# Attention probabilities and values as fp16 parts in every tile, fewer turns by TensorE, and the second expert layer on four column groups

## Chip, cores and metric

The kernel runs on one core of a Trainium2 chip. The metric is the device time of one execution in microseconds (us); the time before is the median of three runs. One core has TensorE (PE; PEld is its load of weights), VectorE (DVE), ScalarE (ACT), GpSimd (POOL), and SyncE (SP), whose queue issues nearly all DMAs, in order. ACT's queue issues some.

## What is computed

Four batches of 576 tokens (2304 in all, 18 tiles of 128) pass through attention with a threshold, a dense layer pair, and a soft mixture of eight experts.

```python
scores = scale * np.matmul(q, k.transpose(0, 1, 3, 2))          # 4 batches, 8 heads, 576 x 576, depth 64
thresh = np.max(scores, axis=-1, keepdims=True) - tau
scores = np.where(scores >= thresh, scores, -1000000000.0)
attn = np.exp(scores - max); attn = attn / (sum + 1e-09)
x = attn @ v                                                    # 2304 x 512
h = x @ w_in; g = np.maximum(0.01 * h, h); x = g @ w_out        # 512 -> 2048 -> 512
logits = x @ phi                                                # 32 slots
slot_input = softmax(logits, 0).T @ x
for e in range(8): slot_out[e] = np.maximum(slot_input[e] @ w1[e], 0) @ w2[e]   # 512 -> 1024 -> 512
out = softmax(logits, 1) @ slot_out
```

## The kernel before

**How the program is ordered.** The code does not issue instructions directly. Each step is added to a plan with its engine or engines, an estimated duration, a priority (about the number of its tile), the buffers it reads and those it writes. A planner then places all steps in one order per engine, by its own estimate of when each can start; buffers are rings of fixed size (the table `O`: `AE`, `AH`, `AT`, `VX`, `VR` and so on are ring sizes, `DP`, `PO`, `PI`, `LH` shift priorities). On the chip each engine runs its list strictly in order. So a changed number in `O` or a changed estimate can move any step.

**Attention of a tile.** `attention(t)` handles 8 heads as 4 pairs. For a pair, `heads` multiplies q by k on PE in fp32 (L1100, two heads side by side on the two halves of the rows), DVE finds the row maxima (L1109) and the threshold (L1115), ACT applies a steep Prelu that drives all below the threshold far down (L1125, L1143). `ends` does the last 64 keys of all heads (L1071). Then there are two ways to get probabilities times values:

- `by_pe`: PE turns the pair's 9 blocks of 128x128 in fp32 (L1159), ACT takes the exponential out of PSUM (L1164), and PE multiplies by the fp32 values (L1176): 10 matmuls for a pair, each of which is two instructions in the trace.
- `by_dma`: ACT takes the exponential in place (L1192), DVE or ACT casts to fp16 (L1202, L1203), POOL writes the rest as a second fp16 part (L1213, three instructions), SP issues two transposing DMAs (L1226), and PE multiplies the fp16 parts by two fp16 parts of the values, `vx` (L1250): 28 matmuls for a pair.

`own` says which pairs go by PE: all four in tiles 0 to 3 (`P0`, `TP=4`), pair 3 in tiles 4 to 17 (`P1`). Tiles 4 and 13 straddle two batches, so their multiplications by values are issued twice. That makes 30 pairs by PE and 42 by DMA.

**The rest of a tile.** The result is scaled, turned (L1295) and split in two fp16 parts; `feed` multiplies by `w_in`, 48 matmuls a tile (L1331), ACT applies the leaky ReLU (L1343), DVE and POOL split the result (L1350, L1357), and four transposing DMAs a tile turn it (L1366) for the logits (L1376, L1380). `w_out` is not applied there: `w_out` times `phi` is made once, at the start (L846, L862), and the first transposing DMAs of `feed` wait for it. Every two tiles `block` adds to the sum over tokens (L1525). The weights arrive as 64-bit numbers and are converted by ACT, DVE and POOL in the first part of the program; values of each batch are scaled and split by `split_v`.

**The experts at the end.** The gather of the slots (L1641) reads `w_out` back from DRAM (16 loads in small buffers, the list `SM`). Then `w1` (32 chunks of 512 KB, L1685) and `w2` (32 chunks, L1753) stream in through the rings that attention no longer needs (`BIG`, 25 buffers here); a chunk's load waits until the matmuls that read the buffer before are done. In the first layer PE goes round the four column groups of 32 (`for j` inside), in the second it does one column group's four matmuls after the other. Then the output is multiplied out (L1785) and stored.

Of the kernel before, what the change touches and what calls it, by code (L numbers as in the profile page):

```python
# [359 lines left out]
def emit(tc, a, out, dbg=None, opt=None):  # L360
# [5 lines left out]
        LH=1.67, LB=3.5, HG=3, NR=6, NT=4, NW=3, XH=1, XT=2, VX=6, AE=2, AH=2, AT=3, QK=8, VS=5,  # L366
        VD=0.3, P0=(0, 1, 2, 3), P1=(3,), TP=4, TX=('eT', 'h'), VR=5, RAW=1, G=2, PO=-4.88,
        PI=-2.55, PV=-9, PK=-8.96, DA=-100, TJ=('rT', 'xT'), PS=0.0, NM=6, E=1, LA=2, MG=800,
        AL=0.44, MH=0, RES=0, MI=(1, 1, 1, 1), MO=(1, 1, 0, 0), WT=('w',), PST=0, BH=1, DP={'vr':
        1.76, 'xT': 0.1, 'xh': 0.34, 'X': 0.29, 'x32': 0.28, 'g': 0.0, 'E': -0.71, 'S0': -0.55,  # L370
        'S1': -1.0, 'h': 1.0, 'r': 1.06, 'rT': 0.34, 'ah': 0.5, 'vx': 0.32, 'misc': -0.82, 'dh':
        -0.87, 'z': -0.89, 'th': 0.68, 'aT': -1.0}, TU=('U', 'rT'), TO=('raw', 'rT'), TG=('g',),
        BI={'spa': 300}, LG=0.06, TE=0.16, NTS=1, WI=('w',), CAP=(), NA=23, QU=(), CX=('aT',),
        TW=('aT', 'g', 'xT'), E2=1, DT=200, TI=('r',), PJ=0.03, NU=2, SM=('vr', 'vx', 'rT', 'w',
        'w2', 'raw', 'x32', 'U'),
# [58 lines left out]
    for n, p_, k in (  # L434
# [4 lines left out]
        ("qk", "main", O["QK"]), ("vr", "main", O["VR"]), ("vx", "main", O["VX"]), ("vs", "main", O["VS"]),  # L439
# [36 lines left out]
    def dump(name, b, sel, prio=1e9):  # L476
        if dbg and name in dbg:
# [36 lines left out]
    gate8, rt = const([P, 1]), const([P, 1])  # L514
    dve_op(
        P0, 80,
        lambda: dve.tensor_scalar(
            out=gate8.ap, in0=gate.ap, scalar1=0.125, scalar2=None, op0=ALU.mult
        ),
        r=[gate], w=[gate8],  # L520
    )
    dve_op(
        P0, 80,
        lambda: dve.tensor_scalar(
            out=rt.ap, in0=taup.ap, scalar1=8.0, scalar2=None, op0=ALU.mult
        ),
        r=[taup], w=[rt],
    )
# [6 lines left out]
    )  # L535

# [289 lines left out]
    for c in range(FF // P):  # L826
# [21 lines left out]
        pe_op(PQ, 440, f, r=[w, ident], w=[tp])  # L848
# [15 lines left out]
        pe_op(PQ, 850, f, r=[wt, phi], w=[wpp])  # L864
# [102 lines left out]
    qk = {}  # L967

    def load_qk(b, prio, step):
        for pr in range(4):  # L970
            raw = qk[b, pr] = pl.buf("qk", [P, 2, KX])
            dma(
                prio + pr * step, t_dma(P * 2 * KX * 4),
                (lambda pr, raw: lambda dq: dq.dma_start(out=raw.ap, in_=a["qk"][b, pr]))(pr, raw), w=[raw],
            )

    vtiles, vfs, vrs_of = {}, {}, {}

    own = lambda t: O["P0"] if t < O["TP"] else O["P1"]
# [25 lines left out]
    def split_v(b, pr, prio, vr):  # L1005
        sv = svs[b]
        vf = lambda: vr.ap[:, :, 0:D]
# [10 lines left out]
        if any(pr not in own(t) for t in tiles_of(b)):  # L1018
            vx = vtiles[b, pr] = pl.buf("vx", [P, 2, 10, D + 2], F16)
            va = lambda w: vx.ap[:, w, :, 0:D]  # L1020
            q = prio + (O["VD"] if any(pr in own(t) for t in tiles_of(b)) else 0.0)
# [13 lines left out]
            fm = lambda eng: lambda: eng.memset(vx.ap[64:, 1, 8:, 0:D], 0.0)  # L1035
            add_alt(q, [("pool", 180, fm(pool)), ("dve", 110, fm(dve))], w=[(vx, 1)])
            for w in range(2):
                pool_op(
                    q, 100, (lambda w: lambda: pool.memset(vx.ap[:, w, :, D : D + 1], 1.0 - w))(w),
                    w=[(vx, 2 + w)],  # L1040
                )
        if any(pr in own(t) for t in tiles_of(b)):
            vs = vfs[b, pr] = pl.buf("vs", [P, 2, D + 2])
            fc = lambda eng: lambda: eng.tensor_copy(out=vs.ap, in_=vr.ap[:, 8:])
            add_alt(prio, [("pool", 300, fc(pool)), ("dve", 150, fc(dve))], r=[vr], w=[vs])
            fm = lambda eng: lambda: eng.memset(vr.ap[:, 0:8, D : D + 1], 1.0)
            add_alt(prio, [("pool", 100, fm(pool)), ("dve", 110, fm(dve))], w=[(vr, 1)])
            fm = lambda eng: lambda: eng.memset(vs.ap[:, :, D : D + 1], 1.0)
            add_alt(prio, [("pool", 100, fm(pool)), ("dve", 110, fm(dve))], w=[vs])
            for i in range(2):  # L1050
                fm = lambda eng, i=i: lambda: eng.memset(
                    vs.ap[64 - 64 * i : 128 - 64 * i, i, 0 : D + 1], 0.0)
                add_alt(prio, [("pool", 100, fm(pool)), ("dve", 110, fm(dve))], w=[vs])
            vrs_of[b, pr] = vr
# [8 lines left out]

    def ends(t, prio):
        Tp = pl.buf(("misc",), [P, H, KT], F32, "Tp")
        Ts, tn = pl.buf("T", [P, H, KT]), pl.buf("tn", [P, H])

        def f():
            for r0, r1, b, o in regs_of(t):
                for pr in range(4):  # L1070
                    pe.matmul(  # L1071
                        out=Tp.ap[r0:r1, 2 * pr : 2 * pr + 2], lhsT=qk[b, pr].ap[:, 0, o : o + r1 - r0],
                        rhs=qk[b, pr].ap[:, 1, KW:KX], start=(pr == 0), stop=True, skip_group_check=True,
                    )

        pe_op(prio, 900 * len(tile_parts(t)), f, r=[qk[b, pr] for b in tile_parts(t) for pr in range(4)], w=[Tp, Ts, tn])
        act_op(prio, t_act(512), lambda: act.activation(out=Ts.ap, in_=Tp.ap, func=AF.Copy), r=[Tp], w=[Ts])
# [5 lines left out]
        dve_op(  # L1083
            prio, 75,
            lambda: dve.tensor_scalar(
                out=tn.ap, in0=tn.ap, scalar1=rt.ap[:, 0:1], scalar2=None, op0=ALU.add
            ),
            r=[rt], w=[tn],
        )
        return Ts, tn  # L1090

    def heads(t, pr, prio, ae, flat, Ts, tn):
# [19 lines left out]
        for i in range(2):  # L1112
# [3 lines left out]
                    out=th.ap[:, i : i + 1], in0=nm.ap[:, i : i + 1], scalar1=rt.ap[:, 0:1],  # L1116
# [13 lines left out]
        tail = lambda: two(ae.ap[:, 2 * KW :]) if flat else ae.ap[:, :, KW:S]  # L1130
        pl.add(
# [15 lines left out]
    def by_pe(t, pr, p, parts, regs, Ts, tn, xa, xbuf):  # L1147
# [5 lines left out]
        def turn(c0, c1, key):  # L1153
# [3 lines left out]
            def f():  # L1157
# [11 lines left out]
        for i, (c0, c1) in enumerate(((0, 4), (4, 8), (8, 9))):  # L1169
            turn(c0, c1, i)  # L1170
# [698 lines left out]
```

## Time and profile before

| | us |
|---|---|
| median of three runs (lowest, highest) | 681.06 (677.28, 685.23) |
| the profiled execution: its time | 686.13 |
| its span, first to last instruction | 684.3 |
| PE, DVE, ACT, POOL busy in the span | 612.7, 406.3, 399.6, 172.8 |
| granted TensorE clock, mean of the span | 0.939 |

The span is read in five stages: up to 60 us loads and the first conversions; from 60 to about 205 us conversions beside the first four tiles; from there to 582 us the steady run of tiles; to 611 us the logits and gather of the last tiles; then the experts. A busy PE is not a PE at its peak, because matmuls overlap: what PE really needs is read from the distance between the starts of matmuls that follow each other at once.

### The profile page before, as it was taken

The page shows a single profiled execution, that of the slowest core. Times are in us where ns is not written, and L with a number is a line of the kernel's source. Part 1 is how long each engine was busy: PE and PEld are TensorE (multiplying, and loading weights), DVE is VectorE, ACT ScalarE, POOL GpSimd, SP SyncE. Part 2 cuts the span into 40 slices and gives each one's busy share as a digit, 9 for nine tenths or more (in the row PEclk, how much of TensorE's full clock was granted, in tenths as well). Part 3 has the DMA queues.
Part 4 walks back from the last instruction along what each step waited for, and adds up shares of the span by engine and source line. Part 5 has one row for each costly group of instructions (what it writes and reads, how often), then busy time and mean ns, then how long its engine had stood idle before and what let it go on. Part 6 is the DMA issues. An engine that isn't in the chain of part 4 may idle for free.

```text
span 684.3 us, 13565 instructions
## 1 busy us (share of the span) xinstructions
PE 612.7 (90%) x5212; PEld 369.2 (54%) x5212; DVE 406.3 (59%) x992; ACT 399.6 (58%) x745; POOL 172.8 (25%) x253
## 2 busy tenths in 40 slices
PE   4898887999879999999999898999999988489995
PEld 1666555776445656565555554655556643224552
DVE  3978869656757586599886555565767343310011
ACT  4887667776747677688786637576666522211022
POOL 0200100200323256245355323263363200200000
PEclk8798988999989999999999889999999999689997
DMA  8965410455998687899697659677669966839995
GB/s 321 375 221 181 129 61 17 139 159 164 163 214 152 115 143 127 186 190 200 121 177 119 114 89 201 132 133 131 105 123 213 203 131 177 267 109 413 409 408 215
DMA packets 203297, 123.94 MB, mean 181 GB/s; under 512 B 179168, under 2 KB 179680, under 8 KB 203232
## 3 DMA queue, kind: packets, MB, share of 16 engines
q1 hardware_dynamic: 199488, 114.02, 69.1%
q10 hardware_dynamic: 3744, 9.05, 5.5%
q8 instruction: 41, 0.67, 0.4%
q14 instruction: 24, 0.20, 0.1%
HBM read 70.48 MB, written 8.91 MB: 116 GB/s over the span
## 4 chain that ended last, share of the span: by engine, by line
PE 69%; ACT 11%; DVE 7%; DMA 6%; issue 3%; SPq 1%; POOL 1%; ACTq 0%; POOLq 0%; DVEq 0%
PE h L1331 23%; PE S L1100 9%; PE X L1176 6%; PE X L1753 6%; PE X L1250 5%; PE eT L1159 3%; PE misc L1176 3%; DMA aT<-ah 2%; ACT e L1164 2%; PE S L1685 2%; DMA rT<-r 2%; PE misc L1071 2%; PE misc L1525 2%; PE misc L862 2%; ACT g L1343 2%
## 5 line engine op out<-in xcount | busy, mean ns | idle before, releaser
L1331 PE MATMUL h<-wh,xT 128*128 128x512 f16 x864 | 215.0, 385 | 7.5 <-ACT g L1343 6.6
L1213 POOL TENSOR_TENSOR ah<-ae,ah 128x512 f16<-128x512 f32 (+1 forms) x126 | 120.6, 984 | 162.3 <-DVE ah L1202 130.7
L1331 PEld LDWEIGHTS <-xT 128*128 128x128 f16 x864 | 80.4, 100 | 101.7 <-issue 35.2
L1125 ACT ACTIVATE ae<-S,th 128x512 f32<-128x512 f32 x144 | 94.3, 686 | 17.5 <-POOL ah L1213 7.0
L1109 DVE TENSOR_REDUCE nm<-S 128x2 f32<-128x1024 f32 x72 | 87.7, 1219 | 28.2 <-PE S L1100 28.1
L1100 PE MATMUL S<-qk 64*128 64x512 f32 (+1 forms) x320 | 89.1, 690 | 9.6 <-DMA qk<-in_qk 5.9
L1343 ACT ACTIVATE g<-h,c 128x512 f32<-128x512 f32 x72 | 49.5, 687 | 70.0 <-PE h L1331 65.0
L1164 ACT ACTIVATE e<-eT,c,c 128x512 f32<-128x512 f32 (+1 forms) x90 | 60.1, 668 | 27.9 <-PE eT L1159 27.8
L1350 DVE CAST r<-g 128x512 f16<-128x512 f32 x57 | 27.8, 487 | 67.4 <-ACT g L1343 62.8
L1250 PEld LDWEIGHTS <-aT 128*128 128x128 f16 (+1 forms) x1344 | 49.7, 103 | 25.0 <-issue 14.6
L1250 PE MATMUL X<-vx,aT 128*128 128x65 f16 (+1 forms) x1344 | 54.4, 196 | 4.5 <-DMA aT<-ah 4.5
L1159 PE MATMUL eT<-c,ae 128*128 128x128 f32 x270 | 49.7, 296 | 8.7 <-ACT e L1164 8.1
L1192 ACT ACTIVATE ae<-ae,c,c 128x1152 f32<-128x1152 f32 x42 | 56.6, 1348 | 0.8
L1159 PEld LDWEIGHTS eT<-c,ae 128*128 128x128 f32 x270 | 34.1, 151 | 28.8 <-ACT e L1164 18.0
L1176 PE MATMUL X<-vr,e 128*128 128x65 f32 (+1 forms) x352 | 47.1, 281 | 0.0
L1357 DVE TENSOR_TENSOR r<-g,r 128x512 f16<-128x512 f32 x56 | 44.3, 791 | 3.9 <-ACT r L1352 3.0
L1134 POOL TENSOR_TENSOR ae<-T,th 128x128 f32<-128x128 f32 x33 | 15.4, 468 | 122.6 <-DVE th L1115 61.4
L1176 PEld LDWEIGHTS X<-vr,e 128*128 128x128 f32 (+1 forms) x352 | 45.0, 200 | 2.3 <-issue 1.2
L1202 DVE CAST ah<-ae 128x1152 f16<-128x1152 f32 x33 | 25.7, 779 | 20.2 <-ACT ae L1192 14.3
L1100 PEld LDWEIGHTS S<-qk 64*128 64x128 f32 (+1 forms) x320 | 23.2, 190 | 26.7 <-ACT ae L1125 7.8
L1115 DVE TENSOR_SCALAR th<-nm,c,tn 128x1 f32<-128x1 f32 x144 | 31.8, 264 | 0.8
L1376 PE MATMUL misc<-c,rT 128*128 128x64 f16 x288 | 19.1, 191 | 9.6 <-DMA rT<-r 9.2
(288 smaller groups left out, 911.0 us busy)
## 6 DMA issues: line engine op xcount, KB each, us to landing
wh<-in_w SPq DMA_DIRECT2D x21, 512.0 KB, 10.1
qk<-in_qk SPq DMA_DIRECT2D x15, 640.0 KB, 5.5
qk<-in_w SPq DMA_DIRECT2D x18, 512.0 KB, 8.0
r<-in_w_in SPq DMA_DIRECT2D x16, 512.0 KB, 4.1
r<-in_w SPq DMA_DIRECT2D x13, 512.0 KB, 10.2
rT<-in_w_out SPq DMA_DIRECT2D x25, 256.0 KB, 3.4
scr<-w SPq DMA_DIRECT2D x16, 256.0 KB, 3.3
vr<-in_v SPq DMA_DIRECT2D x9, 330.0 KB, 4.4
```

What stands on the lines that cost most here:

```text
L1100: pe.matmul(out=ps.ap[r0:r1, i], lhsT=qk[b, pr].ap[h, 0, o : o + r1 - r0], rhs=qk[b, pr].ap[h, 1, 0:KW], start=True, stop=True, skip_group ...
L1109: lambda: dve.tensor_reduce(out=nm.ap, in_=ps.ap, axis=AX.X, op=ALU.max, negate=True),
L1125: (lambda i: lambda: act.activation(out=main()[:, i], in_=ps.ap[:, i], func=AF.Prelu, bias=th.ap[:, i : i + 1], scale=1.0, alpha=2.0**90))(i),
L1159: pe.transpose(tp.ap[:, c - c0], ae.ap[:, c * P : (c + 1) * P], ident.ap)
L1164: lambda: act.activation(out=eT.ap[:, c0:c1], in_=tp.ap, func=AF.Exp, bias=nt.ap[:, 0:1], scale=gate8.ap[:, 0:1]),
L1176: pe.matmul(out=xa(2 * pr + i)[r0:r1], lhsT=eT.ap[:, c, r0:r1], rhs=(vfs[b, pr].ap[:, i] if c == 8 else vrs_of[b, pr].ap[:, c])[:, 0 : D + 1],
L1192: lambda: act.activation(out=ae.ap, in_=ae.ap, func=AF.Exp, bias=nt.ap[:, 0:1], scale=gate8.ap[:, 0:1]),
L1213: lambda: pool.tensor_tensor(out=ah.ap[:, h, w0 : w0 + c1 - c0], in0=ae.ap[:, h, c0:c1], in1=ah.ap[:, h, c0:c1], op=ALU.subtract),
L1250: pe.matmul(out=xa(2 * pr + i)[r0:r1], lhsT=w()[:, r0:r1], rhs=vtiles[b, pr].ap[:, wv, cv, 0 : D + 1], start=(n == 0 and 2 * pr + i in (0, ...
L1331: pe.matmul(out=hp.ap, lhsT=xT.ap[:, wx * 4 + k], rhs=wh(k, j, ww), start=(n == 0), stop=(n == 11),)
L1343: (lambda g, hp, j: lambda: act.activation(out=g.ap, in_=hp.ap, func=AF.Prelu, alpha=0.01, scale=hsc.ap[:, j : j + 1]))(g, hp, j),
L1357: fg = lambda eng, j, g: lambda: eng.tensor_tensor(out=r[j](1), in0=g.ap, in1=r[j](0), op=ALU.subtract)
```

## The change

1. Probabilities and values are now multiplied as fp16 parts in all pairs. `by_pe` has a new kind, "h": after the turn and the exponential, the result is cast to fp16 (DVE or ACT) and its rest is written as a second part (POOL or DVE), in three pieces; then 30 fp16 matmuls a pair (L1335 of the new file) replace the 10 in fp32.
2. Which pair goes which way: `K0='dhdh'` in tiles 0 to 3 (pairs 0 and 2 by DMA, 1 and 3 turned by PE), `K1=('dddd',)` in tiles 4 to 17 (all by DMA). So 8 pairs are turned by PE and 64 by DMA.
3. `split_v` makes `vx` for all pairs of all batches, the small tile `vh` for the "h" pairs, and no fp32 `vs` any more.
4. The second expert layer takes four chunks at a time and goes round the column groups in its inner loop.
5. Nine of the last sixteen chunks of `w1` are loaded as 18 halves into the small buffers (`SM`).
6. Ring sizes, priorities and some estimates changed. Code for splitting q and k in fp16 parts was added, but `QB=9` is above the highest batch, so it never runs (the options `QB`, `QR`, `HT` have no effect on what is computed).

```diff
-        LH=1.67, LB=3.5, HG=3, NR=6, NT=4, NW=3, XH=1, XT=2, VX=6, AE=2, AH=2, AT=3, QK=8, VS=5,
-        VD=0.3, P0=(0, 1, 2, 3), P1=(3,), TP=4, TX=('eT', 'h'), VR=5, RAW=1, G=2, PO=-4.88,
+        HT=0, HF=9, LH=1.9, LB=3.5, HG=3, NR=6, NT=4, NW=3, XT=2, VX=5, AE=2, AH=2, AT=3, QK=8,
+        VS=1, VD=0.52, TP=4, TX=('eT', 'h'), VR=4, RAW=1, G=3, PO=-6.45, PI=-0.91, PV=-8.22, PK=-9,
...
-    own = lambda t: O["P0"] if t < O["TP"] else O["P1"]
+    kind = lambda t, pr: (O["K0"] if t < O["TP"] else O["K1"][t % len(O["K1"])])[pr]
...
+        eh = pl.buf("ah", [P, 2, 9, P], F16)
+        for c0, c1, key in ((0, 4, 0), (4, 8, 1), (8, 9, 2)):
+            n = (c1 - c0) * P
+            pl.add(
+                p2,
+                [
+                    ("dve", P2(t_dve2(n)), lambda c0=c0, c1=c1: dve.tensor_copy(
+                        out=eh.ap[:, 0, c0:c1], in_=eT.ap[:, c0:c1])),
+                    ("act", t_act(n), lambda c0=c0, c1=c1: act.activation(
+                        out=eh.ap[:, 0, c0:c1], in_=eT.ap[:, c0:c1], func=AF.Copy)),
+                ],
...
+            fl = lambda eng, c0=c0, c1=c1: lambda: eng.tensor_tensor(
+                out=eh.ap[:, 1, c0:c1], in0=eT.ap[:, c0:c1], in1=eh.ap[:, 0, c0:c1], op=ALU.subtract)
...
+                todo = [(we, wv, c) for we, wv in ((0, 0), (0, 1), (1, 0)) for c in (*range(4 * i, 4 * i + 4), 8)]
...
+    def w1_of(e, k, late):
+        if not late:
+            w = load(a["w1"][e, k], T0 - 7, [P, 2, 512])
+            return [w, w], lambda n: w.ap[:, n]
+        w = [load(a["w1"][e, k][:, n], T0 - 7.5, [P, 512], "c2", SM, 512) for n in range(2)]
+        return w, lambda n: w[n].ap
...
-                for j in range(4):
-                    q = hts[G]
-
-                    def f(j=j, n=n, G=G, q=q, w=ws[j], hf=hf):
-                        for c in range(4):
+
+                def f(n=n, G=G, ws=ws, hf=hf):
+                    for c in range(4):
+                        for j in range(4):
                             pe.matmul(
```

**Where instructions stand, first place: PE in the first tile.** Before, these are a part of PE's list early in tile 0; `eT` is the turned pair, `S_77` the next pair's scores, `misc<-c_132,w` belongs to `w_out` times `phi`.

```order
L1159 MATMUL eT<-c_83,ae 128x128 x4
L1100 MATMUL S_77<-qk 128x512 x2
L1159 MATMUL eT<-c_83,ae 128x128
L1176 MATMUL X<-vr,e_183 128x65 x4
L1176 MATMUL X<-vs,e_183 128x65
L1176 MATMUL X<-vr,e_183 128x65 x4
L1176 MATMUL X<-vs,e_183 128x65
```

Now the same stretch of PE's list reads as follows (`aT` comes from a transposing DMA).

```order
L1206 MATMUL S_76<-qk 128x512 x2
L891 MATMUL misc<-c_136,w 128x32 x4
L1172 MATMUL misc<-qk 128x128 x4
L1278 MATMUL eT<-c_83,ae 128x128 x4
L1206 MATMUL S_77<-qk 128x512 x2
L875 MATMUL h<-c_83,w 128x128 x4
L1278 MATMUL eT<-c_83,ae 128x128 x4
L1411 LDWEIGHTS aT
L1411 MATMUL X<-vx,aT 128x65
```

The fp32 products are gone; the first product of tile 0 now waits in PE's list for a transposing DMA, behind the scores of three later pairs and beside `w_out` times `phi`.

**Second place: SP's list during the conversions.** Before, SP issues only loads and stores there (`r<-in_w_in` and `rT<-in_w_out` are weights to be converted, `scr<-w` stores converted ones).

```order
L837 DMA scr<-w 128x512
L601 DMA rT<-in_w_out 128x512 x3
L837 DMA scr<-w 128x512
L601 DMA raw<-in_w_out 128x512
L601 DMA rT<-in_w_out 128x512
L837 DMA scr<-w 128x512
L601 DMA rT<-in_w_out 128x512
L601 DMA r<-in_w_in 128x1024
```

Now transposing DMAs of the first tiles stand between them.

```order
L866 DMA scr<-w 128x512
L1387 DMA_TRANSPOSE aT<-ah 128x9x128 x2
L630 DMA r<-in_w_in 128x1024
L866 DMA scr<-w 128x512
L630 DMA raw<-in_w_out 128x512
L630 DMA r<-in_w_in 128x1024 x2
L1387 DMA_TRANSPOSE aT<-ah 128x9x128 x2
L630 DMA r<-in_w_in 128x1024
```

Loads of weights that stood behind loads now also stand behind 16 transposing DMAs, each of which waits for POOL.

**Third place: PE in the second expert layer.** Before, PE's list has the four matmuls of a chunk together.

```order
L1753 MATMUL X<-qk,ae 32x256 x8
L1753 MATMUL X<-qk,ah 32x256 x4
L1753 MATMUL X<-ae,ah 32x256 x4
L1753 MATMUL X<-wh,ah 32x256 x12
L1753 MATMUL X<-r,ah 32x256 x4
```

Now it goes round four chunks, one for each column group.

```order
L1921 MATMUL X<-qk,ae 32x256
L1921 MATMUL X<-e_8481,ae 32x256
L1921 MATMUL X<-qk,ae 32x256 x3
L1921 MATMUL X<-e_8481,ae 32x256
L1921 MATMUL X<-qk,ae 32x256 x3
```

The first matmul of a group of 16 now waits for all four of its chunks.

## Rows read from the trace of the kernel before

**Rows 1.** Stretches: us, busy time (instructions) by engine, granted clock, DMA share, GB/s.
```profile
60.00:120.00 60.00, 47.35 (x256) 33.03 (x254) 48.24 (x116) 41.32 (x74) 5.28 (x8) 0.83 0.27 84
120.00:180.00 60.00, 56.61 (x409) 40.94 (x410) 37.25 (x92) 43.15 (x93) 7.87 (x8) 1.00 0.58 160
...
216.00:369.00 153.00, 151.86 (x1529) 91.19 (x1525) 116.25 (x280) 114.92 (x200) 70.54 (x93) 1.00 0.83 153
369.00:436.00 67.00, 60.66 (x569) 35.19 (x566) 38.51 (x87) 37.56 (x70) 21.77 (x25) 0.90 0.71 131
...
568.00:613.00 45.00, 30.51 (x222) 13.99 (x224) 12.25 (x32) 9.07 (x20) 5.08 (x15) 0.77 0.64 193
613.00:662.00 49.00, 48.47 (x320) 22.70 (x312) 4.40 (x21) 5.71 (x11) 0.00 (x0) 1.00 1.00 396
```

**Rows 2.** The same for line L1331 alone: PE and PEld, 216 to 369 us.
```profile
216.00:369.00 153.00, 70.22 (x288) 25.79 (x288) 1.00 0.83 153
```

**Rows 3.** First and last start of PE's logits matmuls, L1376 (min/median/max ns).
```profile
L1376 PE MATMUL misc<-c,rT x288: 189/189/235, 205.2 to 589.4; 128*128 128x64 f16 x144
```

**Rows 4.** The chain that ended last, 285 to 345 us: start, us, what.
```profile
306.65 1.06 PE misc L1176 x10
307.71 1.06 PE S L1100 x4
...
329.40 0.44 PE X L1250 x14
...
330.49 0.44 PE eT L1159 x4
...
340.26 2.59 PE h L1331 x12
```

**Rows 5.** Costliest groups on the page: out<-in, shapes xcount | busy us, mean ns | idle.
```profile
L1213 POOL TENSOR_TENSOR ah<-ae,ah 128x512 f16<-128x512 f32 (+1 forms) x126 | 120.6, 984 | 162.3 <-DVE ah L1202 130.7
...
L1164 ACT ACTIVATE e<-eT,c,c 128x512 f32<-128x512 f32 (+1 forms) x90 | 60.1, 668 | 27.9 <-PE eT L1159 27.8
...
L1192 ACT ACTIVATE ae<-ae,c,c 128x1152 f32<-128x1152 f32 x42 | 56.6, 1348 | 0.8
...
L1202 DVE CAST ah<-ae 128x1152 f16<-128x1152 f32 x33 | 25.7, 779 | 20.2 <-ACT ae L1192 14.3
```

**Rows 6.** DMA queue over 386 to 398 us, transposes alone: packets, MB, share; landing us.
```profile
q1 hardware_dynamic: 6720, 1.67, 74.1%
...
aT<-ah SPq DMA_TRANSPOSE x3, 3.4
```

**Rows 7.** SP's queue in time, 171 to 216 us: start, us held, what, count.
```profile
172.61 12.88 SPq L1226 DMA_TRANSPOSE aT<-ah  x3
185.53 12.24 SPq L1366 DMA_TRANSPOSE rT<-r  x4
```

**Rows 8.** PE in time, 86 to 100 us: start, us, what, count.
```profile
89.51 1.91 PE L1176 MATMUL X<-vr,e 128*128 128x65 f32 x8
...
98.94 1.06 PE L1176 MATMUL X<-vr,e 128*128 128x65 f32 x8
```

**Rows 9.** The chain that ended last, from 611 us: start, us, what.
```profile
611.17 8.79 PE S L1685 x80
...
632.15 15.95 PE X L1753 x104
...
662.28 9.90 PE X L1753 x80
```

**Rows 10.** SP's queue in time, 560 us to the end: loads of expert weights.
```profile
595.39 2.08 SPq L1673 DMA_DIRECT2D r<-in_w  x4
613.11 3.93 SPq L1673 DMA_DIRECT2D qk<-in_w  x8
...
655.06 1.62 SPq L1673 DMA_DIRECT2D wh<-in_w  x2
```

**Rows 11.** DMA issues from 575 us: KB each, median us to landing.
```profile
r<-in_w SPq DMA_DIRECT2D x13, 512.0 KB, 10.2
```

More of the change, by code (lines that the diff above doesn't have):

```diff
@@ L513, in emit @@
     )
[L514 to L528, printed above, removed]
+    gate8, rt8 = const([P, H]), const([P, H])
+    for o_, i_, f_ in ((gate8, gate, 0.125), (rt8, taup, 8.0)):
+        dve_op(
+            P0, 80,
+            (lambda o_, i_, f_: lambda: dve.tensor_scalar(
+                out=o_.ap, in0=i_.ap.to_broadcast([P, H]), scalar1=f_, scalar2=None, op0=ALU.mult))(o_, i_, f_),
+            r=[i_], w=[o_],
+        )
     dve_op(
@@ L1006, in split_v @@
         sv = svs[b]
+        kinds = set(kind(t, pr) for t in tiles_of(b))
         vf = lambda: vr.ap[:, :, 0:D]
@@ L1062, in regs_of @@
         return [(0, 64, parts[0], S - 64), (64, P, parts[1], 0)]
+    held_T = lambda t: O["HT"] and all(kind(t, pr) == "d" for pr in range(4))
+    pl.early.add("Tq")
+    PROD = ((0, 0), (0, 1), (1, 0))
     def ends(t, prio):
-        Tp = pl.buf(("misc",), [P, H, KT], F32, "Tp")
-        Ts, tn = pl.buf("T", [P, H, KT]), pl.buf("tn", [P, H])
+        still = held_T(t)
+        Tp = pl.buf(("eT",) if still else ("misc",), [P, H, KT], F32, "Tq" if still else "Tp")
+        tn = pl.buf("tn", [P, H])
+        Ts = Tp if still else pl.buf("T", [P, H, KT])
         def f():
@@ L1070, in f @@
                 for pr in range(4):
[L1071 to L1077, printed above, removed]
+                    todo = PROD if fine(b) else (None,)
+                    for n, w in enumerate(todo):
+                        q, k = (qk[b, pr].ap, qk[b, pr].ap) if w is None else (qk[b, pr].ap[:, w[0]], qk[b, pr].ap[:, w[1]])
+                        pe.matmul(
+                            out=Tp.ap[r0:r1, 2 * pr : 2 * pr + 2], lhsT=q[:, 0, o : o + r1 - r0],
+                            rhs=k[:, 1, KW:KX], start=(pr == 0 and n == 0), stop=(n == len(todo) - 1),
+                            skip_group_check=True,
+                        )
+        pe_op(
+            prio, 760 if fine(tile_parts(t)[0]) else 1000, f,
+            r=[qk[b, pr] for b in tile_parts(t) for pr in range(4)], w=[Tp, tn] + ([] if still else [Ts]),
+        )
+        rt = by_rows(prio, t, "rt", lambda b: rtau[b])
+        if not still:
+            act_op(prio, t_act(512), lambda: act.activation(out=Ts.ap, in_=Tp.ap, func=AF.Copy), r=[Tp], w=[Ts])
         dve_op(
@@ L1130, in heads @@
         tail = lambda: two(ae.ap[:, 2 * KW :]) if flat else ae.ap[:, :, KW:S]
+        if held_T(t):
+            for i in range(2):
+                act_op(
+                    prio - 0.01, 232,
+                    (lambda i: lambda: act.activation(
+                        out=tail()[:, i], in_=Ts.ap[:, 2 * pr + i], func=AF.Prelu, bias=th.ap[:, i : i + 1],
+                        scale=1.0, alpha=2.0**90))(i),
+                    r=[Ts, (th, i)], w=[(ae, 2 + i)],
+                )
+            return
         pl.add(
@@ L1170, in by_pe, with f @@
             turn(c0, c1, i)
+        if kind(t, pr) == "f":
+            for i in range(2):
+                def f(i=i):
+                    for r0, r1, b in regs:
+                        for n, c in enumerate((*range(4 * i, 4 * i + 4), 8)):
+                            pe.matmul(
+                                out=xa(2 * pr + i)[r0:r1], lhsT=eT.ap[:, c, r0:r1],
+                                rhs=(vfs[b, pr].ap[:, i] if c == 8 else vrs_of[b, pr].ap[:, c])[:, 0 : D + 1],
+                                start=(n == 0 and 2 * pr + i in (0, H - 1)), stop=(n == 4), skip_group_check=True,
+                            )
+                pe_op(
+                    p + 0.22, 5 * 252, f, r=[(eT, (k, x[0])) for k in (i, 2) for x in regs] + [v[b, pr] for b in parts for v in (vfs, vrs_of)],
+                    w=[xbuf(2 * pr + i)],
+                )
+            return
@@ L1679, in emit @@
         for k in range(4):
-            ws = [load(a["w1"][4 * G + j, k], T0 - 7, [P, 2, 512]) for j in range(4)]
+            ws = [w1_of(4 * G + j, k, G and 4 * k + j >= 16 - O["HF"]) for j in range(4)]
             def f(k=k, ws=ws, h1=h1):
```

265 lines of the change are left out of this document (187 added, 78 removed).

## Prediction

> **What bounds the kernel now.** I read the stretches of the whole span first, then the chain of waits, then the queues. In the steady part, 216 to 369 us, PE is busy 151.86 of 153 us [rows 1], and 288 feed matmuls, six tiles of 48, begin there [rows 2]: 25.5 us a tile. The other columns of the same row, divided by six, give DVE 19.4, ACT 19.2, POOL 11.8 us a tile, and the DMA share of 0.83 gives 21.2. So PE is the limit, and the chain of waits there runs through PE alone; it names the prices [rows 4]: 12 feed matmuls 2.59 us, the scores of a pair 1.06, four fp32 turns 0.44 (nine: 0.98), ten fp32 matmul instructions 1.06 (a pair has twenty: 2.1, or 2.2 with the gaps between), fourteen fp16 matmuls 0.44 (28: 0.88). Added up by such distances between starts, a tile needs 24.0 us: 10.4 feed, 4.2 scores, 3.2 for the pair turned by PE, 2.6 for three pairs by DMA, 3.6 for all the rest. That is 94% of 25.5.
>
> Ahead of the first logits matmul, which starts at 205.2 us [rows 3], there is no one limit. PE is busy 47 of 60 and 57 of 60 us, DVE 48 and 41, ACT 41 and 43 [rows 1], and what the logits wait for, `w_out` times `phi`, is the end of a sequence of loads, conversions, stores and turns that shares all engines with the first four tiles. At the end the loads decide: 396 GB/s at a DMA share of 1.00 from 613 to 662 us, but a share of only 0.64 from 568 to 613 [rows 1], where SP's queue has a hole from 597 to 613 us because all 25 buffers are full [rows 10].
>
> **The change part by part.** All sums are made against the profiled execution's own 686.1 us (span 684.3 and 1.8 around it), 5.1 above the median of 681.06; I subtract 5 at the end.
>
> *The steady body.* The pair of a tile that PE turned goes by DMA. Removed on PE: 0.98 + 2.2 us; added: 0.88. That is 2.3 us, so 24.0 becomes 21.7, and at the same 94% the tile would take 23.1. Removed on ACT are three exponentials of the turned pair, 2.0 us, added one of 1.35; DVE or ACT gets one cast of 0.78; POOL gets three more subtractions of 0.98, 2.95 together [rows 5]. So ACT stands at 18.5, DVE at 20.2, POOL at 14.8: all below 23.1 and hidden by PE. If that cover went, DVE's 0.8 would be the price.
>
> SP gets two more transposing DMAs a tile, eight for six. Each moves 128x1152 fp16, 0.295 MB. Where transposes ran alone, the queue moved 1.67 MB in 74.1% of 12 us [rows 6], 188 GB/s, so one takes 1.57 us of all 16 engines, and two make 21.2 us into 24.3. A plain load runs at 396 GB/s [rows 1], twice that. So DMA, not PE, may be what is late next: 24.3 lies above 23.1. Yet the share of 0.83 counts transfers that slow each other (three transposes that met loads held SP's queue for 12.88 us [rows 7], against 3.4 us to land alone [rows 6]), and part of that gives when there is room. I take 24.0 us a tile, between the two and nearer to the DMA's sum. From 205.2 to 589.4 us [rows 3] there are 384 us, 15.1 tiles, by 1.5: **-22**. Bounds: 23.1 (-36), and 24.8, half way back from 24.3 to now (-10).
>
> The Trainium skill ("Advanced Engine Details and Errata", section X-Bar Transpose) says that transposing DMAs are as fast as regular ones on this chip. By that rule the two would cost 1.5 us a tile, DMA would stand at 22.7, PE's 23.1 would decide and the body would give -36. The trace disagrees: 188 GB/s against 396.
>
> *The ring of two `ah` buffers.* A pair holds one from the cast until its transposes land: 0.78 + 2.95 + 3.4 = 7.1 us, four pairs on two buffers 14 us a tile: hidden. With the landing of 12.9 us of [rows 7] it is 16.6, and 33 us a tile: that would bind.
>
> *The start.* Of the 16 pairs of tiles 0 to 3, eight go by DMA (2.3 us less on PE each, 18) and eight are turned, cast and multiplied in fp16 (0.98 + 30 by 0.44 / 14 = 1.9 us, 1.3 less each, 10). With what the new order moves behind the first logits, some 37 us of PE work less stand ahead of it. Against that DVE has some 10 us more there (casts of 16 pairs at 0.78 between it and ACT, and the split of all values), POOL 16 by 2.95 = 47. PE is not what `w_out` times `phi` waits for alone: DVE, at 48 of 60 us, gets more work. And SP's list, which held only loads and stores, now has 16 transposes between the weights' loads, each waiting for POOL's last part; behind it in the queue stand the loads of `w_in` and `w_out`, for which the converting engines wait. PE's first product now waits for a transpose too, and in PE's list the later scores and turns of `w_out` stand behind it, for which DVE and ACT wait. I take **-2**: relief of PE and new waits about cancel. Bounds: two thirds of 37 (-25); all 16 held as those three, 4.3 us each, unhidden (+69).
>
> *The end.* Eighteen halves, nine chunks of w1, are loaded into the small buffers. A chunk takes 0.524 MB / 396 GB/s = 1.32 us, nine 11.9. They can go into the hole of the queue after the gather has read its buffers; of the hole about 7.5 us can be filled, so -7.5 (-3 to -11). In the second layer, 256-column matmuls that stay in one column group take 15.95 / 104 = 0.153 us; the first layer, which goes round the groups, takes 8.79 / 80 = 0.11 for 512 columns [rows 9], so 0.055 for 256. Now the last load is issued by 656.7 us [rows 10] and lands some 10.2 us later [rows 11], while the chain's last piece of that layer runs from 662.28 for 9.9 us to 672.2 [rows 9]: some 5 behind the landing. After the change the last 32 instructions take 1.8 us (3.5 at the lower clock): -3.5 (-1 to -4). Sum of the end: **-11** (-4 to -15). Faster matmuls ahead of the last gain nothing; loads cover them.
>
> Together: -22 - 2 - 11 = -35, 651 us of its own time, **646** beside the median.
>
> **Rivals.** *A, the queue has room.* Transposes fit between the loads, PE decides at 23.1 us a tile: -36 - 2 - 11 = -49, 632 us. For it: a share of 0.83 is not full, and part of it is collision. Against: 24.3 summed. The skill's rule cited above would bring this case about. Chance 0.13, held low by the 188 GB/s.
>
> *B, PE's relief reaches the start too.* -36 - 25 - 11 = -72, 609 us. For it: PE is busy 57 of 60 us before `w_out` times `phi` is done. Against: DVE and SP get more. Chance 0.12.
>
> *C, the transposing queue binds.* Twelve transposes a tile with the two `ah` buffers late: the body stays at 25.5, the start gets 3 worse: +3 - 11 = -8, 673 us. For it: 24.3 us of DMA at the 94% that PE reaches would be 25.9, and [rows 7]. Chance 0.20: 0.06 of it faster by over 1%, 0.11 within, 0.03 slower.
>
> *D, the other side: SP's queue in the start.* The 16 transposes hold the loads of the weights, 4.3 us each, 69 in all. It decides from 33 / 69, about half unhidden, on; at two thirds it is +45: 686 - 22 - 11 + 45 - 5 = 693 us. Against it: loads are issued ahead by a ring of buffers, and POOL is busy only 5 to 8 of 60 us there, so its parts come soon. Chance 0.08.
>
> *E, TensorE's clock.* From 60 to 120 us, with PE busy 47 of 60, the granted clock is 0.83, so part of it is at 1.2 GHz, and the same eight instructions took 1.91 us at 89.5 us and 1.06 at 98.9 [rows 8]; from 120 to 180 us, busy 57 of 60, it is 1.00 [rows 1]. With 37 us of work taken out, these later 85 us may fall to 0.83 as well: 0.17 by 85 = +14, 660 us. The Trainium skill ("TensorE: Matmul & The Clock Gate", Part 1) says that activity releases the throttle and idleness brings it back; the two stretches agree. Chance 0.07.
>
> **How the numbers follow.** My forecast (637 to 660) has 0.40, A 0.13, B 0.12, C 0.20, D 0.08, E 0.07. About 1% is what a measurement of this kernel can tell from no change. Faster by more than that are the forecast, A, B, E and 0.06 of C: 0.78; within it 0.11 of C; slower D and 0.03 of C: 0.11. The range goes from 606 (below B's time) to 678 (above C's), which leaves out D, the part of C without any gain, and the far end of B, just under 2 in 10.
>
> **What would show it.** Body: the 48 feed matmuls of a tile every 24.0 us instead of 25.5, with PE busy clearly below 99% and the DMA share near 0.95; at A PE stays full at 23.1; at C PE waits for `aT`, or DVE's cast for `ah`. Start: the first logits matmul within some 5 us of 205.2; at B near 180, at D after 235 with SP's queue held for long by transposes, at E with a granted clock below 0.9 between 120 and 180 us. End: loads of halves in the hole before 613 us, and the last matmul of the second layer 2 us after the last landing. The prediction is wrong if PE's work was not the limit of the body, if the halves can't be issued before the gather is done, or if the first product's wait for a transpose holds up what stands behind it in PE's list.

## The result, and the profile after

The changed kernel takes 633.38 us, median of four runs (632.18 to 639.35), against 681.93 of the kernel before: a ratio of 0.931 (95% interval 0.923 to 0.939). Forecast were 646 us and a range of 606 to 678. In a later series the ratio was 0.937 (0.928 to 0.946). The profiled execution of after was the slowest of its four, 639.35 us, so against the 686.13 of the profile before the change is -46.8; the sum had -35. The two spans, 684.3 and 637.3 us, divide at the first and the last start of the logits matmuls:

| us | before | after | change | forecast |
|---|---|---|---|---|
| start, to the first logits matmul | 205.2 | 191.6 | -13.6 | -2 |
| body, first to last logits matmul | 384.2 | 363.8 | -20.4 | -22 |
| end, from there | 94.9 | 81.9 | -13.0 | -11 |

In one more profile of each kernel the same three are 204.8, 383.6, 95.0 and 192.8, 362.1, 81.7: -12.0, -21.5 and -13.3. So the body and the end came about as the sum had them, and the start gave a gain that the sum did not have. How much of that gain belongs to the change is less sure than the table looks: a third profile of the kernel before, below, reaches its first logits matmul at 196.1 us.

These rows answer to [rows 1], [rows 2] and [rows 3]: stretches of the kernel after (us, busy time of PE, PEld, DVE, ACT and POOL with their instructions, granted clock, DMA share, GB/s), then the feed matmuls alone, then the logits line with its first and last start.

```profile
60.00:120.00 60.00, 47.12 (x343) 36.05 (x342) 54.18 (x131) 48.97 (x99) 21.52 (x23) 0.63 0.66 192
120.00:180.00 60.00, 54.72 (x438) 31.84 (x438) 52.41 (x134) 44.44 (x84) 19.04 (x23) 0.91 0.62 158
...
216.00:369.00 153.00, 142.92 (x1520) 77.66 (x1520) 122.12 (x291) 119.29 (x201) 76.65 (x90) 1.00 1.00 176
369.00:436.00 67.00, 64.70 (x756) 35.96 (x757) 52.65 (x114) 45.92 (x78) 37.39 (x44) 1.00 1.00 180
```

```profile
216.00:369.00 153.00, 75.39 (x306) 27.19 (x306) 1.00 1.00 176
```

```profile
L1537 PE MATMUL misc<-c,rT x288: 189/189/236, 191.6 to 555.4; 128*128 128x64 f16 x144
```

In the body PE is no longer full: 142.9 of 153 us against 151.9. The DMA share stands at 1.00, and over 216 to 540 us at 1.03. It adds up the times of all packets and divides by 16 engines, so above 1 some packets overlap: a share of 1 is no ceiling. In that stretch of the kernel after, these are the largest wait of PE and the largest of ACT for an engine other than PE (for PE it waits 42.0 us) (us in total, times, longest):

```profile
PE h L1492 <- ACT g L1504: 12.4, 23, 1.9
```

```profile
ACT ae L1234 <- POOL ah L1374: 21.0, 18, 2.4
```

Before (216 to 568 us) the first was 3.6 us in 6 waits, the second 6.5 in 5. So two small waits stand where PE's removed work was: the next group of feed matmuls waits for ScalarE to empty the one PSUM buffer, and ScalarE waits for POOL, which has all four pairs of a tile to split and holds the two `ae` buffers meanwhile. That the second wait causes the first is not shown. Over the whole run PE waited for the transposes of the probabilities for 0.7 us, as the page's costliest groups tell (busy us, mean ns, then idle before and its releasers):

```profile
L1411 PE MATMUL X<-vx,aT 128*128 128x65 f16 (+1 forms) x1792 | 72.6, 196 | 1.0 <-DMA aT<-ah 0.7
```

The end, as its chain of waits tells it (start, us, what), against [rows 9]:

```profile
589.10 3.57 PE S L1854 x32
592.67 10.17 DMA wh<-in_w
...
602.90 10.16 DMA r<-in_w
...
613.08 10.14 DMA qk<-in_w
...
623.27 1.93 PE X L1921 x26
```

Before, the chain of the end ran through PE in all three rows shown; now it runs through loads, one behind the other, and PE's second layer closes 2 us behind the last landing.

### The profile page after: what moved, and what is told of

The parts are those of the page before. It is cut to its first block, busy times and chain, and to the rows that moved or that the text cites. A ratio compares the mean times of both kernels' runs of the same rounds, so it can differ in the third digit from the quotient of the medians.

```text
span 637.3 us, 13913 instructions
## 1 busy us (share of the span) xinstructions
PE 550.2 (86%) x5286; PEld 309.5 (49%) x5286; DVE 442.8 (69%) x1049; ACT 406.1 (64%) x733; POOL 240.1 (38%) x300
## 5 line engine op out<-in xcount | busy, mean ns | idle before, releaser
L1374 POOL TENSOR_TENSOR ah<-ae,ah 128x512 f16<-128x512 f32 (+1 forms) x192 | 185.5, 993 | 198.8 <-DVE ah L1363 107.5
L1411 PEld LDWEIGHTS <-aT 128*128 128x128 f16 (+1 forms) x2016 | 74.5, 102 | 32.1 <-issue 18.9
L1353 ACT ACTIVATE ae<-ae,c,c 128x1152 f32<-128x1152 f32 x64 | 86.3, 1348 | 1.5
L1411 PE MATMUL X<-vx,aT 128*128 128x65 f16 (+1 forms) x1792 | 72.6, 196 | 1.0 <-DMA aT<-ah 0.7
L1363 DVE CAST ah<-ae 128x1152 f16<-128x1152 f32 x49 | 37.8, 771 | 8.9 <-DMA aT<-ah 3.9
L891 PEld LDWEIGHTS misc<-c,w 128*128 128x128 f32 x128 | 24.6, 285 | 14.5 <-ACT w L881 5.2
L891 PE MATMUL misc<-c,w 128*128 128x32 f32 x128 | 26.1, 362 | 4.4 <-ACT w L881 3.4
L1172 PE MATMUL misc<-qk 128*128 128x128 f32 (+1 forms) x160 | 23.8, 305 | 1.7 <-ACT T L1184 1.4
L1172 PEld LDWEIGHTS misc<-qk 128*128 128x128 f32 (+1 forms) x160 | 20.8, 201 | 6.6 <-issue 3.2
L1262 ACT ACTIVATE ae<-ae 128x128 f32<-128x128 f32 x72 | 22.5, 314 | 1.5 <-DVE ae L1253 1.5
```

Source lines behind the costliest of these rows:

```text
L891: pe.matmul(out=wpp.ap, lhsT=wt.ap[:, k], rhs=phi.ap[:, k], start=(k == 0), stop=(k == 3))
L1172: pe.matmul(out=Tp.ap[r0:r1, 2 * pr : 2 * pr + 2], lhsT=q[:, 0, o : o + r1 - r0], rhs=k[:, 1, KW:KX], start=(pr == 0 and n == 0), stop=(n ...
L1353: lambda: act.activation(out=ae.ap, in_=ae.ap, func=AF.Exp, bias=nt.ap[:, 0:1], scale=rs.ap[:, 2 * pr : 2 * pr + 1]),
L1363: ("dve", P2(t_dve2(2 * S)), lambda: dve.tensor_copy(out=ah.ap[:, :, :S], in_=ae.ap)),
L1374: lambda: pool.tensor_tensor(out=ah.ap[:, h, w0 : w0 + c1 - c0], in0=ae.ap[:, h, c0:c1], in1=ah.ap[:, h, c0:c1], op=ALU.subtract),
L1411: pe.matmul(out=xa(2 * pr + i)[r0:r1], lhsT=w()[:, r0:r1], rhs=vtiles[b, pr].ap[:, wv, cv, 0 : D + 1], start=(n == 0 and 2 * pr + i in (0, ...
```

## Experiments

Unless said otherwise an experiment is the changed kernel with one edit, and is compared with it by the three stretches above and by medians (633.4 and 634.9 us in its two series). Its profile lies 6.0 us above its median, so differences of medians come out some 5 us larger than those of spans. The experiments ran on three chips, on which the kernel before had medians of 674.7, 676.5 and 682.6 us; only the two runs on the first four tiles have their reference on the same chip, so the stretches are the firmer evidence. In the five profiles whose order is the changed kernel's up to the first logits matmul (the two without an edit, and those with more PE work in the body, the old second layer and no halves), that matmul starts at 189.6 to 192.8 us.

**More PE work in the body.** In `feed`, with the order of all steps unchanged:

```diff
+                        for _ in range(3 if n == 0 and t >= 4 else 0):
+                            pe.matmul(out=hp.ap, lhsT=xT.ap[:, wx * 4 + k], rhs=wh(k, j, ww), start=True, stop=True)
                         pe.matmul(
```

> The changed kernel with three more feed matmuls ahead of each group of twelve in tiles 4 to 17; each starts its sum anew, so the output is the same and no step moves. 14 tiles x 4 groups x 3 = 168 matmuls at 0.2155 us are 36 us of TensorE work, 2.6 us a tile. Theory P (TensorE paces the body of the changed kernel): +27 to +36 us, some 662 to 670 us beside 633. Theory Q (the transposing DMA queue paces it at about 24 us a tile, as the forecast had it): TensorE has 1 to 2 us a tile to spare, so +5 to +18 us.

662.57 us (661.3 to 663.24). Its logits line:

```profile
L1542 PE MATMUL misc<-c,rT x288: 189/189/235, 190.9 to 579.8; 128*128 128x64 f16 x144
```

The body is 388.9 us, 25.1 longer for 36 us of matmuls, 0.7 us for each; start and end stay within a microsecond, and the medians differ by 28 to 29. The total is in the range of theory P and far above that of Q: PE sets most of the pace, not all of it. The matmuls were added inside the groups that share the one PSUM buffer; the same work in another place was not tried.

**More DMA work in the body.**

```diff
-                (lambda aT, i: lambda: sp.dma_start_transpose(out=aT.ap, in_=ah.ap[:, i]))(aT, i),
+                (lambda aT, i: lambda: (sp.dma_start_transpose(out=aT.ap, in_=ah.ap[:, i]), probe(t, pr, i)))(aT, i),
...
+    def probe(t, pr, i):
+        if t >= 4 and i == 0:
+            sp.dma_start(out=spare[4 * t + pr], in_=a["w1"][t % 8, pr][:, 0])
```

> The changed kernel with one extra copy of 256 KB, DRAM to DRAM, on SP's queue behind the first transposing DMA of each pair of tiles 4 to 17: 56 copies, 14.7 MB, about 37 us of queue time at 396 GB/s, 2.6 us a tile; nothing reads the copies and no step moves. Theory Q (the DMA queue paces the body): +25 to +40 us. Theory P (TensorE paces it, the queue has room): 0 to +10 us.

656.2 us (652.65 to 662.33).

```profile
L1543 PE MATMUL misc<-c,rT x288: 189/189/216, 189.2 to 572.4; 128*128 128x64 f16 x144
```

Body 383.2 us, 19.4 longer for 37 us of copies (an estimate, at 396 GB/s): 0.5 us for each. That lies between the two theories: the queue is not free in the body either. From 200 to 350 us the share is 1.12, above the 1.00 that was taken for full. And PE now does wait for the transposes, from 216 to 560 us. The stretch in the changed kernel and here, then that wait:

```profile
200.00:350.00 150.00, 139.94 (x1529) 77.10 (x1527) 118.89 (x282) 113.56 (x193) 73.05 (x88) 1.00 1.01 179
```

```profile
200.00:350.00 150.00, 134.89 (x1440) 73.57 (x1438) 110.14 (x263) 106.03 (x183) 69.64 (x81) 0.98 1.12 207
```

```profile
PE X L1417 <- DMA aT<-ah: 8.1, 6, 4.8
```

**One pair of each later tile turned by PE again, in fp16.**

```diff
-K1=('dddd',)
+K1=('dddh',)
```

> The changed kernel with pair 3 of tiles 4 to 17 turned by TensorE and multiplied in fp16 (kind h) instead of by DMA. TensorE gets 0.98 + 0.94 - 0.88 = 1.04 us more a tile, SP two transposes less a tile, 3.1 us of the sixteen engines' time. Theory P: +10 to +16 us. Theory Q: -5 to -20 us.

658.65 us (656.84 to 659.33). Its logits line, the stretch and a wait of PE:

```profile
L1537 PE MATMUL misc<-c,rT x288: 189/189/261, 185.8 to 575.8; 128*128 128x64 f16 x144
```

```profile
200.00:350.00 150.00, 139.67 (x1528) 79.87 (x1526) 118.69 (x274) 110.71 (x200) 64.55 (x79) 0.99 0.79 149
```

```profile
PE eT L1456 <- DVE x L1447: 6.8, 5, 2.4
```

Body 390.0 us, 26.2 longer, where 14 x 1.04 = 15 us of PE work were added and 14 x 3.1 = 44 us of transposes were taken from the queue. Theory Q falls: the DMA share from 200 to 350 us goes from 1.01 to 0.79, and that gives nothing back. Theory P has the sign, not the size. From 216 to 560 us PE now waits 6.8 us for DVE ahead of the turn of a tile's result, against 0.8 before the edit, so part of the rest is other engines' work that a turned pair brings; how much the planner's other order adds was not separated.

**The kernel before, with its pair 3 by DMA from tile 9 on.**

```diff
-    own = lambda t: O["P0"] if t < O["TP"] else O["P1"]
+    own = lambda t: O["P0"] if t < O["TP"] else O["P1"] if t < 9 else ()
```

> The kernel before with one edit: in tiles 9 to 17 pair 3 goes by DMA as well, all else as before (start, end, priorities). Nine tiles lose 2.3 us of TensorE work each, 21 us. Theory P: -17 to -24 us. Theory Q (24.0 us a tile for 25.5): -9 to -14 us. If the gain of the change were in its new priorities and not in the kinds: -5 to +5 us.

670.7 us, median of ten (662.45 to 694.21), against 676.52 of the kernel before on that chip (665.57 to 693.16): ratio 0.997 (0.991 to 1.004), which tells nothing apart from no change. The trace tells more:

```profile
L1376 PE MATMUL misc<-c,rT x288: 189/189/236, 196.1 to 564.2; 128*128 128x64 f16 x144
```

The body is 368.1 us in this profile, 16.1 below the kernel before, for nine tiles: 1.8 us a tile, of 2.3 that PE lost. That is near theory P. But the profile is of a run of 662.45 us, 8 below the median, and 9.1 us of its lead lie in the start, which the edit does not touch. The medians are 5.8 us apart, the lowest times (662.45 and 665.57) 3.1: they do not bear theory P out, and as totals they lie in or near the -5 to +5 of the rival that the new priorities give the gain. So by this run that rival is not excluded.

**The kernel before once more.** No edit.

> The kernel before once more, unaltered, to see in which stage its runs, 665 to 693 us, differ. If the differences lie in the start (granted clock of TensorE there): the first logits matmul moves between 193 and 207 us and the stretch from there to the last logits matmul stays within 3 us of 384. If they lie in the body: that stretch moves by 5 us or more.

686.69 us, median of four (675.03 to 694.55). The profiled run is of 685.19 us:

```profile
L1376 PE MATMUL misc<-c,rT x288: 189/189/236, 204.8 to 588.4; 128*128 128x64 f16 x144
```

All three stretches are those of the first profile within 0.6 us, but this run happened to last as long (685 and 686 us), and the two starts are equal by chance. The run before this one tells it: up to 187 us every engine has the order of the kernel before, and its first logits matmul comes at 196.1 us. Against it this run is 8.0 us behind when the second tile's x is turned (112.3 us; 104.3 there, 105.0 in the first profile), after a granted clock of 0.60 from 20 to 60 us (0.80 there, 0.91 in the first profile). The first profile is still level when the third tile's x is turned (141.7 and 141.1 us) and 5.7 us behind at the fourth (194.4 and 188.7). In between three transposes of the probabilities land only after 13.2, 17.0 and 14.4 us (10.1, 10.5 and 5.7 in the other run), and from 176 to 206 us of the first profile PE waits for them, as it does not in the other run:

```profile
PE X L1250 <- DMA aT<-ah: 4.5, 2, 2.6
```

So the start alone makes runs of this kernel differ by 9 us. What makes up the rest of their 4% stays open.

**The changed kernel once more.** No edit; it is the reference of the two runs on the first four tiles.

> The changed kernel once more, unaltered, on the same chip as the next three, as their reference: 630 to 640 us, first logits matmul at 189 to 193 us.

634.93 us (632.52 to 638.68).

```profile
L1537 PE MATMUL misc<-c,rT x288: 189/189/235, 192.8 to 554.9; 128*128 128x64 f16 x144
```

**Start: more VectorE work.** Each maximum over w_in is taken twice, in the same place:

```diff
-                (lambda k, raw, am=am: lambda: dve.tensor_reduce(...))(k, raws[k]),
+                (lambda k, raw, am=am: lambda: [dve.tensor_reduce(...) for _ in range(2)])(k, raws[k]),
```

> The changed kernel with the 16 maxima over w_in taken twice on VectorE (same result, no step moves): 16 x 0.675 = 10.8 us more VectorE work, all in the start. Theory V (VectorE sets the start): +8 to +11 us. Theory W or K (TensorE sets it): 0 to +4 us.

642.28 us (639.14 to 646.9). First logits matmul at 199.0 us, 7.4 and 6.2 later than in the two profiles of the changed kernel, for 10.8 us of work: 0.6 to 0.7 us for each.

```profile
L1537 PE MATMUL misc<-c,rT x288: 189/189/237, 199.0 to 560.1; 128*128 128x64 f16 x144
```

**Start: more PE work, and a warmer clock.** Every turn of a w_out chunk four times over:

```diff
-            for k in range(4):
+            for k in (*range(4), *range(4), *range(4), *range(4)):
                 pe.transpose(tp.ap[:, k], w.ap[:, k * P : (k + 1) * P], ident.ap)
```

> The changed kernel with every turn of a w_out chunk done four times over (16 matmuls for 4, same result, no step moves): 192 more matmuls by 0.109 us, 21 us of TensorE work at full clock, up to 42 at half, all before 170 us. The granted clock there is 0.56 to 0.67 from 20 to 120 us. Theory K (the half clock, which came with the relief of PE, ate the start's gain): clock above 0.8 and the first logits matmul at 180 to 192 us, total -10 to 0 us. Theory W (TensorE's work is still on the path of the start): +10 to +25 us. Theory V (VectorE and ScalarE set the start, TensorE waits for them): 0 to +6 us, whatever the clock.

647.29 us (645.87 to 647.58). Its stretches of the start, and the logits line:

```profile
20.00:60.00 40.00, 30.03 (x204) 21.92 (x202) 34.48 (x80) 30.93 (x60) 12.90 (x19) 0.80 0.90 279
60.00:120.00 60.00, 44.58 (x402) 37.42 (x402) 51.74 (x121) 46.14 (x93) 21.43 (x23) 0.83 0.69 188
```

```profile
L1537 PE MATMUL misc<-c,rT x288: 189/189/237, 195.9 to 560.1; 128*128 128x64 f16 x144
```

The granted clock rises from 0.56 and 0.63 to 0.80 and 0.83, and the first logits matmul comes at 195.9 us, 4.3 later, not sooner. So theory K falls as it was put: at a clock above 0.8 the mark does not come early. What the higher clock gave back and what the 21 us of added PE work cost can't be told apart here; together they cost 4.3. With the doubled maxima this points to VectorE, more than PE, as what paces the start of the changed kernel; ScalarE was not tested. The medians differ by 12 to 14 us, which is theory W's range, but only 4.3 of it lie in the start; 3.5 lie in the end (85.4 us instead of 81.9), which no edit touched, and why is open.

**Start: the first four tiles in fp32 by PE, as before.**

```diff
-K0='dhdh'
+K0='ffff'
...
-VS=1
+VS=5
```

> The changed kernel with tiles 0 to 3 as before: all 16 pairs turned and multiplied in fp32 by TensorE (and five vs buffers, which that needs). TensorE gets 8 x 2.3 + 8 x 1.3 = 29 us more ahead of the first logits matmul, VectorE about 10 us less. Theory V (VectorE sets the start, 0.7 us per us by the doubled maxima; TensorE 0.2 by the repeated turns): -7 + 6, so -4 to +4 us. Theory W (TensorE sets it, the step as the kernel before had it): +15 to +29 us.

672.85 us (664.74 to 681.99), 38 above the changed kernel on the same chip, more than either theory allowed; its lowest time is still 30 above. The profile is of the run of 681.99 us. Stretches, then the logits line, then DVE's part of turning a tile's x, of which the fourth tile's is the last up to 235 us:

```profile
60.00:120.00 60.00, 52.03 (x220) 43.58 (x219) 44.38 (x106) 36.46 (x77) 3.06 (x4) 0.50 0.54 171
```

```profile
L1537 PE MATMUL misc<-c,rT x288: 189/189/233, 168.6 to 600.4; 128*128 128x64 f16 x144
```

```profile
L1465 DVE TENSOR_TENSOR xT<-eT,xT x3: 691/691/692, 102.6 to 229.7; 128x512 f16<-128x512 f32 x3
```

With less on VectorE the first logits matmul comes 23 us sooner (168.6 us), but the fourth tile's x is turned at 229.7 instead of 194.8 us, and the body grows by 68, with only 63 feed matmuls ahead of the mark where the changed kernel has 120. In the new order PE's fp32 work is on the path: 52 of 60 us busy at a granted clock of 0.50; what it would cost at the higher clock this run does not tell. So theory V holds at most for the changed kernel, with PE relieved, and not for this one. The first logits matmul alone would have told a gain here.

**Start: all 16 pairs by DMA.**

```diff
-K0='dhdh'
+K0='dddd'
```

> The changed kernel with all 16 pairs of tiles 0 to 3 by DMA: 16 more transposes among the loads on SP's queue; TensorE 8 us less, ScalarE 5 us less, VectorE some 8 us less (the rests of the turned pairs that it wrote). Theory V: -4 to -8 us. Theory D (the forecast's rival: transposes among the loads hold SP's queue, 4.3 us each): 16 x 4.3 = 69 us if all unhidden, at least +10.

639.11 us (637.46 to 640.27), 4 above its reference; first logits matmul at 191.8 us (reference 192.8). Sixteen more transposes among the loads cost nothing up to that mark. The fourth tile's x is turned 4.6 us later (200.7 and 196.1 us), the seventh no later (275.0 and 275.8), so rival D's mechanism has no price here that lasts. Theory V's gain did not come either: the total is a little longer, in the profiles by 1.7 us, which lie in the end (84.0 and 81.7 us), and that was not followed up.

**End: the old order of the second layer.**

```diff
-                    for c in range(4):
-                        for j in range(4):
+                    for j in range(4):
+                        for c in range(4):
```

> The changed kernel with the second expert layer's old order: one column group's four matmuls after the other. The forecast's step: the last 32 instructions take 32 x 0.153 = 4.9 us instead of 1.8, and PE lags the loads by more: +3 to +4 us, the last matmul 5 to 6 us behind the last landing instead of 2. Rival: the order is worth nothing, since PE waits for loads (0 to +1 us).

640.4 us (636.32 to 647.52). Start and body are those of the changed kernel within a microsecond, the end is 89.8 us, 7.9 longer. The chain of waits:

```profile
594.77 4.39 PE X L1921 x32
...
600.19 11.68 PE X L1921 x96
...
615.84 4.52 PE X L1921 x32
...
621.87 11.68 PE X L1921 x96
```

The last load lands at 623.4 us, as in the changed kernel (623.2), but the layer ends at 633.55, 10 us behind it. The medians differ by 5.5 to 7.0 us. So the new order is worth up to twice what was expected: at 0.12 to 0.14 us for each instruction of the old one, PE had fallen behind well before the last group.

**End: no halves.**

```diff
-HF=9
+HF=0
```

> The changed kernel without halves: all of w1 in whole chunks into the large buffers. The forecast's step: the queue's hole before the first expert matmul comes back, +7.5 us (3 to 11), with no loads of w1 for some 8 to 12 us before the large buffers come free. Rival: the loads were bound by something else, for instance by when the large buffers come free of attention, 0 to +2 us.

643.83 us (640.98 to 644.27). SP's queue of loads:

```profile
556.52 1.75 SPq L1834 DMA_DIRECT2D r<-in_w  x4
574.13 1.28 SPq L1834 DMA_DIRECT2D qk<-in_w  x3
```

The hole is back, 558.3 to 574.1 us, and the DMA share from 555 to 580 us is 0.49 instead of 0.89. The end is 91.0 us, 9.1 longer than with halves, and its last 26 instructions again take 1.93 us behind the last landing. The body is 361.0 us, where the two profiles of the changed kernel have 363.8 and 362.1.

## Why the prediction was right or wrong

**Body: right in size, right in the first cause, wrong in the limit it chose.** That PE was the bound and that the turned pair's work would come out of it holds in the profiles: PE's busy time between the two logits marks falls from 364.3 to 338.5 us (-26), and the time by 20.4; from 216 to 369 us 306 feed matmuls begin instead of 288, 24.0 us a tile, as forecast. But 24.0 was put between PE and the transposing queue. Taking transposes away gave nothing back, and PE waited 0.7 us for them in all, so the queue's 24.3 was no limit, and that 24.0 was hit is luck: it is 22.4 us of busy PE and 1.6 us without work, not a queue. The step that failed is the one that took share times time (21.2 us a tile) for work under a ceiling, since the share goes to 1.03 here and to 1.12 with the copies. PE's busy part of the stretch goes from 95% to 93%, which is where the other 5 us of the 26 went; the waits for ScalarE shown above grew by 9 us beside it. Transfers are not free either: added copies cost half their queue time. How much of the 20.4 us the new priorities and rings brought was not separated; the kernel before with nine tiles changed gained 16.1 in its profile's body and 5.8 by medians.

The rate of 188 GB/s for transposes alone [rows 6] was not what decided. The Trainium skill ("Advanced Engine Details and Errata", section X-Bar Transpose) has them as fast as regular DMAs; no run here changes the 188 against 396 that the trace of before shows, and case A's time came about without that rule being borne out.

**Start: the step "relief of PE and new waits about cancel" fell short, by how much is open.** -2 was taken, -13.6 and -12.0 came. But the kernel before has 196.1 us in its third profile, against which the changed kernel's 189.6 to 192.8 are 3 to 7 us of gain; so some 9 us of the -13.6 can be what the two runs of the kernel before lost, one after a stretch at a lower clock, one waiting for transposes. `w_out` times `phi` is finished sooner (last and first starts of its matmuls, against 173.3 us before), and the feed begins later, at 123.5 us against 59.8:

```profile
L891 PE MATMUL misc<-c,w x128: 192/401/422, 28.3 to 162.9; 128*128 128x32 f32 x128
```

The fourth tile's x, however, is turned at 194.8 us, against 194.4 before (188.7 in the third profile). So what gain there is seems to lie in the order, which puts `w_out` ahead of the feed; no run has that order alone. It rests on the fp16 products in the first four tiles: with fp32 there the total is 38 us longer. PE's busy time in the start fell by 15 us (148.9 to 133.8 from 30 us on), while its granted clock went from 0.92 to 0.75. VectorE, at 54 and 52 of 60 us, is now the fuller of the two from 60 to 120 us, and 0.6 to 0.7 us came for each us added to it. The prediction did name VectorE as what would be late.

**End: right, its two terms of the wrong size.** -11 forecast, -13 measured. The halves are worth 9.1 us in the presence of the other edit, with 7.5 said; the order of the second layer 7.9 (5.5 to 7.0 by medians), with 3.5 said. The step that failed is "faster matmuls ahead of the last gain nothing; loads cover them". With the old order PE closed 10 us behind the last landing instead of 2. Both are worth more than the whole, 17.0 against 13.0 (14.6 with the order's lower figure), so each alone is worth less, if nothing else moved the end (13.0 - 7.9 = 5.1 for the halves, 13.0 - 9.1 = 3.9 for the order, near the 3.5 said): earlier loads need a PE that keeps up, and a faster PE needs loads that come.

**The rivals.** A's time of 632 us was met within 2, but not by its sum (-36, -2, -11 against -20, -14, -13). That the forecast of 646 is 13 off and the range still holds the result owes much to the width of the range. B, PE's relief in the start, came about by little more than half at most. C and D fall: no wait for a transpose binds in the changed kernel, and neither 16 nor 32 of them held its start. E's mechanism appeared, earlier than said: the granted clock is 0.63 from 60 to 120 us (before 0.83) and 0.91 from 120 to 180 (before 1.00). What it cost is open, since the run with the higher clock had added work too. That more activity lifts the clock is what the Trainium skill ("TensorE: Matmul & The Clock Gate", Part 1) says, and the run with the repeated turns agrees: with 204 and 402 PE instructions instead of 158 and 343 in the two stretches, the clock goes from 0.56 and 0.63 to 0.80 and 0.83. PE's busy share does not tell it: that fell in the same two stretches.

## What to carry to other kernels

Work taken off the engine that is full comes back as time only until the next wait: here 20 of 26 us in the body. A probe that adds a known amount of work to one engine, with the order of all steps kept, gives the rate for each engine and stage. Two profiles of one kernel that agree do not show that it always takes that time: here they agreed by two different losses, and a third was 9 us shorter. A DMA share below 1 is not the room that is left, nor one near 1 a limit: test it by adding and by taking away. Two edits at one place, earlier loads and a faster reader, are to be costed together, since each by itself may be worth a third of the pair.

## What the runs showed of the hardware that was not expected

The DMA share, the sum of the packets' times over 16 engines, went above 1, to 1.12 from 200 to 350 us in the run with added copies, with more bytes moved (207 GB/s against 179 without them).

The granted clock of a stretch is not fixed by the program: the kernel before had 0.91 from 20 to 60 us in one profile and 0.60 in the other, with PE busy 36.2 and 38.1 of 40 us. The one at 0.60 turned the second tile's x 7.3 us later than the one at 0.91, and 8.0 later than a third run at 0.80. And the clock was 0.50 from 60 to 120 us, the lower level throughout, with PE busy 52 of 60 us (the run with fp32 in the first four tiles).

The same three transposes of 128x1152, in the same order, landed after 13.2, 17.0 and 14.4 us in one run of the kernel before and after 10.1, 10.5 and 5.7 in another.

A matmul of 32 weight columns by 256 took 0.12 to 0.15 us a piece while the matmuls stayed in one column group, and 1.93 / 26 = 0.074 where they went round four, at the end of the second layer.
